# Paired landmark work, casts by DMA and earlier block sums in a fused attention and feed-forward kernel

## The chip, the cores and the metric

The kernel runs on one core of one Trainium2 chip. The metric is the device time in microseconds (us) of one execution; a profiled execution also has a span, from its first to its last recorded work. "PE" is TensorE, "PEld" its weight loads, "DVE" VectorE, "ACT" ScalarE, "POOL" GpSimd and "SP" SyncE, whose queue issues DMAs.

## The reference

Two stages. The first is an attention of eight batches, eight heads, 576 rows and 64 columns by landmarks (each the mean of 18 rows), with an iterated inverse:

```python
q_lm = q.reshape(B, H, 32, 18, D).mean(axis=3)
k_lm = k.reshape(B, H, 32, 18, D).mean(axis=3)
A, Bm, C = sm(q, k_lm), sm(q_lm, k_lm), sm(q_lm, k)   # softmax of scaled scores
Z = Bm.T / (norm1(Bm) * norminf(Bm) + 1e-06)          # per head
for _ in range(6):
    Z = 2 * Z - Z @ Bm @ Z
x = A @ Z @ C @ v                                     # heads side by side: (8, 576, 512)
```

The second takes `u = x + real(fft(fft(x, axis=1), axis=2))`, normalizes each row of u, and returns `u + max(un @ w_ch1, 0) @ w_ch2`, with w_ch1 of 512 x 2048 and w_ch2 of 2048 x 512.

## The kernel before

**Order of work.** The program first writes down every instruction as an `Op` with an assumed duration, a phase, a group and the tiles it touches (`Order.op`). `Order.solve` then plays the engines through in simulated time: on each engine the ready instruction with the smallest phase goes first, within a phase and batch the one with the longest chain behind it. The resulting order is issued as it stands, all of it through one line (L1324), which is why every row of the profile names that line; groups are told apart by tile names. Additions and subtractions issued through `self.E` may go to DVE or POOL, as the planner finds room.

**Tiles.** Buffers come from pools (`SLOTS`, L85; `BANKS`, L84). In the pools of `IN_ORDER`, "big" (8 tiles of 1280 columns) among them, a tile is given out only in the order in which the program wrote its uses down, whatever the phases say. "row" has 6 tiles; PSUM has 4 banks named "at", of which 2 are held for good from chunk 4 on. Two of the big tiles are held from then on as well, as a ring for block sums.

**Attention** (`attention`, L678) handles one batch in two groups of four heads. It loads k and q (two big tiles each), reduces them to landmark sums `lm` and a masked copy `qbd`, splits q into two fp16 halves, and calls `landmarks` (L943). That computes `Bm` for the eight heads, its norms, and six iterations (a bundle of 16 products of 32x32 blocks, a copy on ACT and an addition on DVE each); between them it calls `keys` and `values`, or from batch 2 (`LATE`) on `keys_turned` and `values_turned`, for C and C @ v. Their result becomes `Wx` and `Wt`. Then come A in three parts, its transposes by DMA, a transform over the rows, and `mix` (L1070), which forms u; `norm` (L1128) makes un and sends it through a DMA transpose into `unT`. Phases are 0 for batch 0 and 100 b for batch b.

**Feed-forward.** Two tiles of 128 rows are a chunk; a batch gives four tiles, and two batches a ninth from what is left. `chunk` (L1166), for chunks 0 to 3, multiplies by w1 (192 products into "hp", phase 1001) and by w2 (into "acc", phase 1000). All operands are two fp16 halves, three products for one. From chunk 4 (`SEVEN`) on `seven` (L1236) replaces the product with w2 by seven products of half blocks, for which `blocks_of` (L1204, phase 1000) has formed sums of w2's blocks and stored them in DRAM. The products of chunks fill whatever time attention leaves on PE. Until the first one, the planner fills PE with dummy products (`hp<-ones`).

**Weights** (`weights`, L597) are unpacked from 64-bit words to 16 tiles each: two ACT instructions, one DVE instruction, a product on PE for the scale, then scaling to `ws`, a cast to the high half (ACT) and a subtraction for the low half.

The block sums depend on one instruction, kept as `self.second`:

```python
if b == 1:
    self.second = self.order.ops[-1]
...
elif chunks == SEVEN - 1: self.order.gate = (self.second,)
```

Of the kernel before, what the change touches and what calls it, by code (L numbers as in the profile page):

```python
# [87 lines left out]
LINK, PATIENCE = 0.05, 0.0  # L88
SEVEN, RING, LATE, PORT, SPARE = 4, 10, 2, 0.05, 0.1
# [343 lines left out]
class Kernel:  # L433
# [77 lines left out]

    def turn(self, out, src):
# [84 lines left out]
    def weights(self):  # L597
# [7 lines left out]
        for w in range(2):  # L605
            gram = self.new("acc")
            for f in range(NF):
# [9 lines left out]
                half = dst.bitcast(BF16).rearrange("p (m x) -> p m x", x=2)[:, :, 1]  # L617
# [26 lines left out]
                for f2 in range(NF) if w else range(4 * g, 4 * g + 4):  # L644
# [6 lines left out]
                    self.A.copy(hi, src)  # L651
# [26 lines left out]
    def attention(self, b):  # L678
# [11 lines left out]
        lm = self.small([P, 2, 128], "lm", bufs=1)  # L690
        am = self.small(4, "amax")
        qbd = self.small([P, 4, 64], "qbd", bufs=1)
        qhs = []
        for g in range(2):
            kf, qf = loads[g][0][:, 0 : 2 * S], loads[g][1][:, 0:NQ]
            V.tensor_reduce(lm[:, g, 64:128], kf.rearrange("p (m t) -> p m t", t=18), AX.X, ALU.add)
            lv = lm[:, g, 0:64].rearrange("p (x o m) -> p x o m", o=2, m=8)
            qv = qf.rearrange("p (x o t) -> p x o t", o=2, t=2 * SEG)
            for o in range(2):
                V.tensor_reduce(lv[:, :, o], qv[:, :, o, o : o + 144].rearrange("p x (m t) -> p x m t", t=18), AX.X, ALU.add)  # L700
            qhs.append(self.big().bitcast(F16))
            A.activation(qhs[g][:, 0:NQ], qf, AF.Abs, accum_out=am[:, g : g + 1])
            V.tensor_tensor(
                qbd[:, 2 * g : 2 * g + 2].rearrange("p r (x m) -> p r x m", x=2),
                lm[:, g, 0:64].rearrange("p (r m) -> p r m", r=2).unsqueeze(2).broadcast_to([P, 2, 2, 32]),
                self.mask2.unsqueeze(1).unsqueeze(3).broadcast_to([P, 2, 2, 32]), ALU.mult,
            )
# [31 lines left out]
        land = self.landmarks(b, loads, qbd, lm)  # L739
# [77 lines left out]
        self.mix(b, ATs, CS, *land())  # L817

# [124 lines left out]
    def landmarks(self, b, loads, qbd, lm):  # L943
        mm, tr = self.mm, self.tr
        V, A = self.V, self.A
        small = self.small
        flat = lambda t: t.rearrange("p a b -> p (a b)")
        Bd = small([P, 2, 32], "Bd")
        R = small([P, 2, 64], "R")
        ps = self.at()  # L950
        self.together()
        for g in range(2):
            for pr in range(2):
                mm(ps[64 * pr : 64 * pr + 64, 32 * g : 32 * g + 32], qbd[:, 2 * g + pr], lm[:, g, 64 + 32 * pr : 96 + 32 * pr])
        self.apart()
        V.tensor_scalar(Bd.rearrange("p g m -> p (g m)"), ps[:, 0:64], 1.0 / 2592.0, None, ALU.mult)
        mx = small(2, "bmx")
        V.tensor_reduce(mx, Bd, AX.X, ALU.max)
        V.tensor_tensor(Bd, Bd, mx.unsqueeze(2).broadcast_to([P, 2, 32]), ALU.subtract)
        A.activation(Bd, Bd, AF.Exp)  # L960
        bs = small(2, "bs")
# [3 lines left out]
        nrm = small([P, 2, 3, 32], "nrm", bufs=1)  # L965
        V.tensor_tensor(nrm[:, :, 1, :], Bd, bs.unsqueeze(2).broadcast_to([P, 2, 32]), ALU.mult)
        rs = small(2, "rs")
        V.tensor_reduce(rs, nrm[:, :, 1, :], AX.X, ALU.add)
        V.tensor_tensor(
            nrm[:, :, 2, :], self.diag32.unsqueeze(1).broadcast_to([P, 2, 32]),  # L970
            rs.unsqueeze(2).broadcast_to([P, 2, 32]), ALU.mult,
        )

        Cs = self.keys(loads, qbd, lm) if b < LATE else self.keys_turned(loads, lm)

        psn = self.at()
        mm(psn[:, 0:128], flat(self.ones_bd), nrm[:, :, 1:3].rearrange("p g x m -> p g (x m)"))
        cm = small(4, "cm")
        V.tensor_reduce(cm, psn[:, 0:128].rearrange("p (x m) -> p x m", m=32), AX.X, ALU.max)
        ci = small(2, "ci")  # L980
# [4 lines left out]
        nci = small(2, "nci")  # L985
        V.tensor_scalar(nci, ci, -1.0, None, ALU.mult)
        BT = small([P, 2, 32], "BT", bufs=1)
        for g in range(2):
            V.transpose(BT[:, g], nrm[:, g, 1, :])
# [3 lines left out]
        for g in range(2):  # L993
# [3 lines left out]
        for g in range(2):  # L997
            V.scalar_tensor_tensor(nrm[:, g, 0, :], pse[:, 32 * g : 32 * g + 32], nci[:, g : g + 1], self.diag32, ALU.mult, ALU.add)
        (self.values if b < LATE else self.values_turned)(loads, Cs, ci, R)

        ES = nrm[:, :, 0:2].rearrange("p g x m -> p g (x m)")
        for it in range(6):
# [3 lines left out]
            for g in range(2):  # L1006
# [289 lines left out]
    def run(self):  # L1296
# [95 lines left out]
```

## Time and profile before

| | us |
|---|---|
| median of 3 runs | 958.4 (956.04 to 960.85) |
| the profiled execution | 957.02 |
| its span | 955.2 |
| PE busy | 923.6 (97%) |
| DVE busy | 760.7 (80%) |
| ACT busy | 490.1 (51%) |
| POOL busy | 225.1 (24%) |
| DMA | 128.27 MB, mean 134 GB/s |

PE's instructions overlap, so its busy time counts the end of one together with the start of the next; a bundle's cost is better read from its start to the start of what follows. An idle time in brackets is the engine's own, and the name behind it is what ended it. Busy shares over the whole span are means over stages of different kinds: weights and batch 0 (to about 70 us), weights with the first chunk, batch 1, block sums with batch 2, then seven-product chunks with attention beside them, and at the end chunks alone.

### The profile page before, as it was taken

The numbers are of one execution on the slowest core, as the hardware profiler recorded it, in microseconds if no ns is written. First come the engines' busy times: TensorE is split into PE (matmuls) and PEld (weight loads), VectorE is DVE, ScalarE is ACT, GpSimd is POOL, SyncE is SP. The second block draws the span as 40 slices with busy tenths as digits, with TensorE's granted clock in tenths as the row PEclk, the third lists the DMA queues.
The fourth block names the chain that finished last, engine by engine and source line by source line (L and its number), as shares of the span: only waits on it lengthen the run. The fifth ranks groups of instructions, "written<-read, shape, count | busy, mean of one in ns | idle before, by whom it ended". The sixth has DMA issues, their size and how long they took to land.

```text
span 955.2 us, 26527 instructions
## 1 busy us (share of the span) xinstructions
PE 923.6 (97%) x10730; PEld 747.6 (78%) x10730; DVE 760.7 (80%) x2012; ACT 490.1 (51%) x1031; POOL 225.1 (24%) x270
## 2 busy tenths in 40 slices
PE   8879899989999999999999999999999999999997
PEld 6668557656566888878888878888888888888886
DVE  7888996898998688898789987997698856865455
ACT  5899853245555444455454534564454633433332
POOL 0322010353552222140314211221242411301010
PEclk9999999999999999999999999999999999999999
DMA  9976110653735571557335552455535433334231
GB/s 347 302 245 210 58 33 17 161 128 79 258 116 149 110 200 54 155 118 197 108 100 155 136 168 66 119 142 134 178 101 155 121 87 95 101 116 116 79 106 50
DMA packets 166795, 128.27 MB, mean 134 GB/s; under 512 B 86416, under 2 KB 155536, under 8 KB 166544
## 3 DMA queue, kind: packets, MB, share of 16 engines
q1 hardware_dynamic: 166672, 126.57, 46.6%
q8 instruction: 84, 1.38, 0.6%
q14 instruction: 39, 0.32, 0.1%
HBM read 94.15 MB, written 14.68 MB: 114 GB/s over the span
## 4 chain that ended last, share of the span: by engine, by line
PE 65%; DVE 8%; DMA 4%; issue 1%; ACT 1%; SPq 1%; POOL 0%; DVEq 0%; ACTq 0%
PE hp L1324 30%; PE at L1324 19%; PE acc L1324 16%; DVE row L1324 2%; DMA big<-big 2%; DMA big<-q_dram 1%; DMA big<-sums 1%; DVE h L1324 1%; DVE big L1324 1%; SPq L1324 1%; DVE u L1324 1%; DVE lm L1324 1%; DVE sum L1324 1%; DMA big<-k_dram 1%; ACT big L1324 0%
## 5 line engine op out<-in xcount | busy, mean ns | idle before, releaser
L1324 PE MATMUL hp<-unT,w 128*128 128x256 f16 x3264 | 389.8, 273 | 0.6 <-DVE h L1324 0.6
L1324 PEld LDWEIGHTS <-w 128*128 128x128 f16 (+1 forms) x3584 | 343.3, 98 | 54.1 <-DVE w L1324 6.9
L1324 PEld LDWEIGHTS <-h 128*128 128x128 f16 x2604 | 247.7, 98 | 66.3 <-DVE h L1324 6.8
L1324 PE MATMUL acc<-w,h 128*128 128x256 f16 (+1 forms) x1260 | 199.3, 294 | 5.0 <-DVE h L1324 3.7
L1324 ACT ACTIVATE ws<-hp 128x512 f32<-128x512 f32 x112 | 66.8, 596 | 170.3 <-PE hp L1324 169.9
L1324 DVE TENSOR_TENSOR sum<-ws 128x256 f32<-128x256 f32 (+1 forms) x272 | 97.2, 402 | 71.4 <-ACT ws L1324 70.7
L1324 ACT CAST h<-sum 128x640 f16<-128x640 f32 x112 | 81.2, 725 | 79.2 <-DVE sum L1324 64.8
L1324 PE MATMUL at<-big,h 128*128 128x256 f16 x672 | 110.1, 273 | 0.0
L1324 POOL TENSOR_TENSOR sum<-ws 128x256 f32<-128x256 f32 (+1 forms) x64 | 44.2, 708 | 221.9 <-ACT ws L1324 193.6
L1324 DVE TENSOR_TENSOR h<-sum,h 128x640 f16<-128x640 f32 x86 | 71.4, 830 | 16.5 <-ACT h L1324 15.9
L1324 POOL TENSOR_TENSOR h<-sum,h 128x640 f16<-128x640 f32 x26 | 36.4, 1402 | 86.3 <-ACT h L1324 86.3
L1324 PE MATMUL acc<-big,h 128*128 128x256 f16 x336 | 55.0, 273 | 0.0
L1324 PE MATMUL at<-w,h 128*128 128x256 f16 x336 | 55.0, 273 | 0.0
L1324 ACT CAST row<-row 128x256 f16<-128x256 f32 (+1 forms) x76 | 36.6, 502 | 32.8 <-DVE row L1324 24.9
L1324 DVE TENSOR_REDUCE lm<-big 128x32 f32<-128x576 f32 (+1 forms) x48 | 44.3, 945 | 11.2 <-DMA big<-k_dram 8.1
L1324 PEld LDWEIGHTS <-big 128*128 128x128 f16 (+1 forms) x768 | 40.1, 99 | 9.0 <-issue 3.7
L1324 ACT CAST h<-ws 128x256 f16<-128x256 f32 x112 | 45.3, 405 | 2.8
L1324 DVE SCALAR_TENSOR_TENSOR u<-at,scw,row 128x128 f32<-128x128 f32 (+3 forms) x120 | 39.0, 387 | 7.8 <-PE at L1324 7.6
L1324 DVE TENSOR_TENSOR h<-ws,h 128x256 f16<-128x256 f32 x98 | 42.7, 435 | 0.4 <-ACT h L1324 0.4
L1324 ACT ACTIVATE big<-big 128x1168 f16<-128x1168 f32 (+1 forms) x26 | 25.4, 988 | 28.2 <-DMA big<-q_dram 18.6
L1324 DVE SCALAR_TENSOR_TENSOR u<-acc,winv,u 128x512 f32<-128x512 f32 x50 | 35.5, 742 | 4.4 <-PE acc L1324 4.3
L1324 POOL TENSOR_TENSOR r<-ve,mhalf 128x2 f32<-128x2 f32 (+1 forms) x20 | 15.6, 782 | 93.8 <-DVE ve L1324 93.5
(226 smaller groups left out, 1331.9 us busy)
## 6 DMA issues: line engine op xcount, KB each, us to landing
big<-sums SPq DMA_DIRECT2D x336, 128.0 KB, 2.2
w<-w_dram SPq DMA_DIRECT2D x22, 512.0 KB, 8.4
big<-q_dram SPq DMA_DIRECT2D x16, 584.0 KB, 6.0
big<-k_dram SPq DMA_DIRECT2D x16, 576.0 KB, 5.9
out_dram<-u SPq DMA_DIRECT2D x36, 256.0 KB, 2.3
big<-v_dram SPq DMA_DIRECT2D x12, 512.0 KB, 4.9
big<-w_dram SPq DMA_DIRECT2D x10, 512.0 KB, 6.2
sums<-row SPq DMA_DIRECT2D x40, 128.0 KB, 1.9
```

Source lines behind the costliest of these rows:

```text
L1324: getattr(engine, name)(*map(real, args), **{k: real(x) for k, x in kw.items()})
```

## The change

`landmarks` is divided. The sums of q and k become `landmark_sums`; Bm, the norms and the six iterations become `normed`, which takes one batch or two and lays them side by side in every tile; what is left of `landmarks` takes its result and runs keys and values behind it. `run` calls `ahead(3, 4)`, `ahead(5, 6)` and `ahead(7)` before batch 2, 4 and 6. `ahead` loads k and q of its batches (phase 100 b - 150, with b the first of them), forms their sums, and runs `normed` (phase 100 b - 50); the tiles of k and q are given back, and `attention` loads both again for its other uses. Batches 0 to 2 do the same work alone. Some small tiles have other numbers of buffers or move to "row".

In `weights`, the high half of every third tile of w1 is cast by a DMA issued on POOL's queue; for w2 the two unpacking instructions write in place of the raw words, and only the third writes the final tile. The block sums depend on the last instruction of batch 0.

```diff
+PULL, DRAW, PAIRS = 150, 50, (3, 5, 7)
...
+    def cast(self, out, src):
+        n = math.prod(src.shape) * mybir.dt.size(src.dtype)
+        self.order.op("POOL", 1.0, 2.3, [out], [src], (self.nc.gpsimd, "dma_start", (out, src), {}), nbytes=n)
...
-                dst, mag = slots[w][f], low.bitcast(F32) if w else self.new("h")[:, 0:512]
-                x = dst.bitcast(I32)
+                dst = slots[w][f].bitcast(I32)
+                x, mag = (low, top.bitcast(F32)) if w else (dst, self.new("h")[:, 0:512])
...
-                V.scalar_tensor_tensor(x, mag.bitcast(I32), 3, x, ALU.logical_shift_left, ALU.bitwise_or)
+                V.scalar_tensor_tensor(dst, mag.bitcast(I32), 3, x, ALU.logical_shift_left, ALU.bitwise_or)
...
-                    self.A.copy(hi, src)
+                    (self.A.copy if w or f2 % 3 else self.cast)(hi, src)
...
-        lm = self.small([P, 2, 128], "lm", bufs=1)
-        am = self.small(4, "amax")
-        qbd = self.small([P, 4, 64], "qbd", bufs=1)
+        am = self.small(4, "amax", bufs=4)
+        alone = b not in self.lms
+        if alone:
+            lm, qbd = self.landmark_sums(loads)
+        else:
+            lm = self.lms[b]
...
+        if alone:
+            self.normed_of[b] = (0, *self.normed([(lm, qbd)]))
...
-            AT = (self.mid(512).bitcast(F16) if u < 2 else self.small(256, "AT2", F16)).rearrange("p (c t) -> p c t", t=P)
-            hl = self.row(1024, F16) if u < 2 else self.small(256, "hl2", F16)
+            AT = (self.mid(512).bitcast(F16) if u < 2 else self.small(256, "AT2", F16, bufs=1)).rearrange("p (c t) -> p c t", t=P)
+            hl = self.row(1024, F16) if u < 2 else self.small(256, "hl2", F16, bufs=1)
...
+    def ahead(self, *batches):
+        b = batches[0]
+        self.set(100 * b - PULL, b, 2.0)
+        found = [self.landmark_sums(self.load(x)) for x in batches]
+        self.lms.update(zip(batches, (lm for lm, _ in found)))
+        self.set(100 * b - DRAW, b, 2.0)
+        made = self.normed(found)
+        for i, x in enumerate(batches):
+            self.normed_of[x] = (2 * i, *made)
+
+    def landmark_sums(self, loads):
+        lm = self.small([P, 2, 128], "lm", bufs=3)
+        qbd = self.row(256).rearrange("p (r m) -> p r m", r=4)
...
+    def normed(self, lms):
+        mm, V, A, small = self.mm, self.V, self.A, self.small
+        n = 2 * len(lms)
...
         for it in range(6):
             c0 = 0 if it < 5 else 32
             ps = self.at()
             self.together()
-            for g in range(2):
+            for g in range(n):
                 for i in blocks:
                     mm(ps[i, 64 * g + c0 : 64 * g + 64], ES[i, g, 0:32], ES[i, g, c0:])
             self.apart()
-            pv = ps[:, 0:128].rearrange("p (g m) -> p g m", g=2)
-            new = small([P, 2, 64], "ES", bufs=3)
+            pv = ps[:, 0 : 64 * n].rearrange("p (g m) -> p g m", g=n)
             if it < 5:
+                new = small([P, 2, 64], "ES", bufs=2) if n == 2 else self.row(256).rearrange("p (g m) -> p g m", g=4)
                 A.copy(new[:, :, 0:32], pv[:, :, 0:32])
...
+    def landmarks(self, b, loads, lm, x, last, ci, keys, values):
+        last, ci = last[:, x : x + 2], ci[:, x : x + 2]
+        values(loads, keys(), ci, R)
...
         for b in range(self.NB):
+            if b + 1 in PAIRS:
+                self.ahead(*range(b + 1, min(b + 3, self.NB)))
             self.attention(b)
-            if b == 1:
+            if b == 0:
                 self.second = self.order.ops[-1]
```

## Rows read from the trace of the kernel before

**Rows 1.** The page of the profile: the span, the busy time of each engine, and the TensorE clock in 40 equal slices (tenths of full speed).

```profile
span 955.2 us, 26527 instructions
...
PE 923.6 (97%) x10730; PEld 747.6 (78%) x10730; DVE 760.7 (80%) x2012; ACT 490.1 (51%) x1031; POOL 225.1 (24%) x270
...
PEclk9999999999999999999999999999999999999999
```

**Rows 2.** Busy time by stage. Columns: stretch in us from the span's start, its length, then the busy us (and instructions) of PE, PE's weight loads, DVE, ACT and POOL, the granted clock, the mean busy share of the DMA engines, GB/s.

```profile
72.00:112.00 40.00, 36.30 (x344) 29.98 (x342) 35.36 (x81) 36.60 (x70) 5.93 (x7) 0.97 0.53 159
112.00:192.00 80.00, 79.48 (x842) 49.04 (x842) 65.48 (x172) 35.73 (x79) 13.57 (x15) 0.98 0.26 67
192.00:300.00 108.00, 102.18 (x1183) 67.81 (x1180) 99.12 (x265) 54.81 (x135) 48.47 (x60) 1.00 0.51 144
300.00:945.00 645.00, 641.59 (x7506) 551.58 (x7504) 495.69 (x1297) 303.04 (x622) 141.86 (x167) 1.00 0.45 123
```

**Rows 3.** TensorE in order of time, 56 to 130 us: start, duration, what, and in brackets the idle time before it and what ended it. The first row is the first multiplication of chunk 0; the last is the first product with w2.

```profile
70.87 8.38 PE L1324 MATMUL hp<-unT,w 128*128 128x256 f16 x60
...
94.51 0.41 PE L1324 MATMUL acc<-w 128*128 128x128 bf16 x4 [0.61 <-DVE w L1324]
...
111.92 3.02 PE L1324 MATMUL acc<-w,mt 128*128 128x512 f16 x6 [1.48 <-ACT w L1324]
```

**Rows 4.** The same view, 120 to 310 us: two products of h with w2 in chunk 1.

```profile
196.83 2.33 PE L1324 MATMUL acc<-w,h 128*128 128x512 f16 x10 [1.18 <-DVE h L1324]
...
201.86 2.33 PE L1324 MATMUL acc<-w,h 128*128 128x512 f16 x10 [1.33 <-DVE h L1324]
```

**Rows 5.** ScalarE in order of time, 36 to 76 and 76 to 130 us: the casts of w1's tiles 0 (46.17), 2 and 3 (50.32), two later ones with the instruction behind them, and tile 12's (86.96).

```profile
46.17 0.61 ACT L1324 CAST w<-ws 128x512 f16<-128x512 f32 x1
...
50.32 1.16 ACT L1324 CAST w<-ws 128x512 f16<-128x512 f32 x2
...
67.54 1.12 ACT L1324 CAST w<-ws 128x512 f16<-128x512 f32 x2
68.57 0.67 ACT L1324 ACTIVATE big<-big 128x512 f32<-128x512 f32 x1
...
86.96 0.63 ACT L1324 CAST w<-ws 128x512 f16<-128x512 f32 x1
```

**Rows 6.** DMA issues by kind: out<-in, queue, operation, count, KB of each, median us from issue to landing.

```profile
sums<-row SPq DMA_DIRECT2D x40, 128.0 KB, 1.9
...
big<-k_dram SPq DMA_DIRECT2D x16, 576.0 KB, 5.9
```

**Rows 7.** Groups of instructions by shape (the sums of a batch's q, its k, and the masked copy): count, busy us, mean ns of one, idle time of the engine before them.

```profile
L1324 DVE TENSOR_REDUCE lm<-big 128x32 f32<-128x576 f32 x32 | 23.0, 745 | 3.0 <-DMA big<-q_dram 3.0
...
L1324 DVE TENSOR_REDUCE lm<-big 128x64 f32<-128x1152 f32 x16 | 21.5, 1347 | 8.2 <-DMA big<-k_dram 8.1
...
L1324 DVE TENSOR_TENSOR qbd<-lm,mask 128x128 f32<-128x128 f32 x16 | 5.7, 370 | 0.1
```

**Rows 8.** The same view: the additions of the iteration, five per batch.

```profile
L1324 DVE TENSOR_TENSOR ES<-ES,at 128x64 f32<-128x64 f32 x40 | 8.4, 210 | 3.5 <-ACT ES L1324 2.4 <-PE at L1324 0.9
```

**Rows 9.** TensorE in order of time: one bundle of the iteration and what follows it (219.85), a bundle of 24 products with Wt (41.72) and a doubled one (260.59), each with what follows.

```profile
219.85 0.43 PE L1324 MATMUL at<-ES 32*32 32x64 f32 x16
220.21 4.11 PE L1324 MATMUL hp<-big,w 128*128 128x256 f16 x36
...
41.72 0.57 PE L1324 MATMUL at<-t,Wt 64*32 64x262 f16 x24
42.23 0.28 PE L1324 MATMUL hp<-ones 128*128 128x256 f16 x1
...
260.59 0.86 PE L1324 MATMUL at<-t,Wt 64*32 64x262 f16 x48
261.38 1.48 PE L1324 MATMUL hp<-unT,w 128*128 128x256 f16 x12
```

**Rows 10.** Groups by shape: the larger parts of the block sums (the sum of a tile's halves, sums of its blocks, their low halves), on VectorE and on GpSimd.

```profile
L1324 DVE TENSOR_TENSOR row<-row 128x256 f16<-128x256 f32 x23 | 12.8, 573 | 0.2 <-ACT row L1324 0.2
...
L1324 POOL TENSOR_TENSOR row<-row 128x256 f16<-128x256 f32 x17 | 12.0, 716 | 23.6 <-ACT row L1324 23.6
...
L1324 POOL TENSOR_TENSOR ws<-w 128x512 f32<-128x512 f16 x11 | 14.3, 1309 | 0.1
...
L1324 POOL TENSOR_TENSOR row<-ws,ws 128x256 f32<-128x256 f32 x15 | 11.7, 782 | 9.4 <-ACT ml L1324 5.4 <-DVE ws L1324 3.9
...
L1324 DVE TENSOR_TENSOR row<-ws,ws 128x256 f32<-128x256 f32 x9 | 3.9, 458 | 0.0
```

**Rows 11.** The SyncE queue in order of time, 0 to 320 us: the first and the last load of k and q of batch 2, and the transpose of its first tile of un.

```profile
178.03 0.57 SPq L1324 DMA_DIRECT2D big<-k_dram  x1
...
185.05 0.42 SPq L1324 DMA_DIRECT2D big<-q_dram  x1
...
283.30 1.28 SPq L1324 DMA_TRANSPOSE unT<-row  x1
```

**Rows 12.** TensorE in order of time: the first multiplication of chunk 4 (each chunk has 192, counted from 70.87).

```profile
301.39 2.79 PE L1324 MATMUL hp<-unT,w 128*128 128x256 f16 x24
```

**Rows 13.** SyncE's transpose of batch 3's rest tile, and TensorE's product that reads batch 2's.

```profile
304.97 1.20 SPq L1324 DMA_TRANSPOSE AT<-hl  x1
...
311.43 0.44 PE L1324 MATMUL at<-Wx,AT 64*64 64x64 f16 x16
```

More of the change, by code (lines that the diff above doesn't have):

```diff
@@ L510, in dma @@
         self.order.ops[-1].name = "dma"
+    def cast(self, out, src):
+        n = math.prod(src.shape) * mybir.dt.size(src.dtype)
+        self.order.op("POOL", 1.0, 2.3, [out], [src], (self.nc.gpsimd, "dma_start", (out, src), {}), nbytes=n)
+        self.order.ops[-1].name = "dma"
     def turn(self, out, src):
@@ L689, in attention @@
         NQ = 16 * SEG
-        lm = self.small([P, 2, 128], "lm", bufs=1)
-        am = self.small(4, "amax")
-        qbd = self.small([P, 4, 64], "qbd", bufs=1)
+        am = self.small(4, "amax", bufs=4)
+        turned = b >= LATE
+        alone = b not in self.lms
[3 more added lines that the diff above has]
+            lm = self.lms[b]
         qhs = []
         for g in range(2):
[L695 to L700, printed above, removed]
-            qhs.append(self.big().bitcast(F16))
[L702 to L707, printed above, removed]
+            qhs.append(self.big().bitcast(F16))
+            A.activation(qhs[g][:, 0:NQ], loads[g][1][:, 0:NQ], AF.Abs, accum_out=am[:, g : g + 1])
         V.tensor_reduce(am[:, 2:4], lm[:, :, 64:128], AX.X, ALU.add, apply_absolute_value=True)
@@ L737, in attention @@
             V.tensor_copy(scr[64 * g : 64 * g + 64], sc[64 * g : 64 * g + 64, 4 + g : 5 + g])
-        land = self.landmarks(b, loads, qbd, lm)
+        if alone:
+            self.normed_of[b] = (0, *self.normed([(lm, qbd)]))
+        if not turned:
+            land = self.landmarks(b, loads, lm, *self.normed_of[b], lambda: self.keys(loads, qbd, lm), self.values)
+        else:
+            land = self.landmarks(b, loads, lm, *self.normed_of[b], lambda: self.keys_turned(loads, lm), self.values_turned)
         aes = []
@@ L817, in attention @@
         self.mix(b, ATs, CS, *land())
+    def ahead(self, *batches):
[8 more added lines that the diff above has]
+    def landmark_sums(self, loads):
+        V = self.V
+        lm = self.small([P, 2, 128], "lm", bufs=3)
+        qbd = self.row(256).rearrange("p (r m) -> p r m", r=4)
+        for g in range(2):
+            kf, qf = loads[g][0][:, 0 : 2 * S], loads[g][1][:, 0 : 16 * SEG]
+            V.tensor_reduce(lm[:, g, 64:128], kf.rearrange("p (m t) -> p m t", t=18), AX.X, ALU.add)
+            lv = lm[:, g, 0:64].rearrange("p (x o m) -> p x o m", o=2, m=8)
+            qv = qf.rearrange("p (x o t) -> p x o t", o=2, t=2 * SEG)
+            for o in range(2):
+                V.tensor_reduce(lv[:, :, o], qv[:, :, o, o : o + 144].rearrange("p x (m t) -> p x m t", t=18), AX.X, ALU.add)
+            V.tensor_tensor(
+                qbd[:, 2 * g : 2 * g + 2].rearrange("p r (x m) -> p r x m", x=2),
+                lm[:, g, 0:64].rearrange("p (r m) -> p r m", r=2).unsqueeze(2).broadcast_to([P, 2, 2, 32]),
+                self.mask2.unsqueeze(1).unsqueeze(3).broadcast_to([P, 2, 2, 32]), ALU.mult,
+            )
+        return lm, qbd
     def keys(self, loads, qbd, lm):
@@ L984, in landmarks @@
         V.reciprocal(ci, ci)
-        nci = small(2, "nci")
+        nci = several(1, "nci")
         V.tensor_scalar(nci, ci, -1.0, None, ALU.mult)
-        BT = small([P, 2, 32], "BT", bufs=1)
-        for g in range(2):
+        BT = small([P, 4, 32], "BT", bufs=1)
+        for g in range(n):
             V.transpose(BT[:, g], nrm[:, g, 1, :])
@@ L992, in landmarks @@
         self.together()
-        for g in range(2):
+        for g in range(n):
             for i in blocks:
@@ L996, in landmarks @@
         self.apart()
-        for g in range(2):
+        for g in range(n):
             V.scalar_tensor_tensor(nrm[:, g, 0, :], pse[:, 32 * g : 32 * g + 32], nci[:, g : g + 1], self.diag32, ALU.mult, ALU.add)
-        (self.values if b < LATE else self.values_turned)(loads, Cs, ci, R)
         ES = nrm[:, :, 0:2].rearrange("p g x m -> p g (x m)")
@@ L1005, in landmarks @@
             self.together()
-            for g in range(2):
+            for g in range(n):
                 for i in blocks:
@@ L1018, in landmarks @@
             self.E.tensor_tensor(
[L1019 removed]
+                nbd[:, g].rearrange("p i (d m) -> p i d m", d=2), last[:, g].unsqueeze(1).unsqueeze(1).broadcast_to([P, 4, 2, 32]),
                 self.mask4.unsqueeze(2).unsqueeze(3).broadcast_to([P, 4, 2, 32]), ALU.mult,
```

57 lines of the change are left out of this document (30 added, 27 removed).

## The prediction

> **What bounds the kernel now.** I read the busy line and the clock slices first, then the stages, then TensorE's (PE's) waits in each stage. PE is busy 923.6 of 955.2 us and its clock stays at the upper level, 2.4 GHz, nearly throughout [rows 1]. The stage table says where the rest lies. PE's idle time is 3.7 us in 72 to 112, 0.5 in 112 to 192, 5.8 in 192 to 300 and 3.4 in the 645 us from 300 to 945 [rows 2]: 13.4 us in all. Before that, PE fills with dummy products until the first multiplication of a chunk at 70.87 [rows 3]; nothing behind it can be done earlier than that point allows. So the kernel after 70.87 is a PE queue that hardly ever runs dry. DVE with 77% and ACT with 47% of the last long stage [rows 2] are not the bound; their saved microseconds count only where PE waited for them. The price of this change is therefore read from 72 to 300, plus whatever it takes out of PE's own queue.
>
> Two waits stand in that stretch. In 72 to 112 ACT is busy 36.6 of 40 us [rows 2], unpacking and splitting the weights, and PE waits for it: 0.61 for an unpacked tile at 94.51 and 1.48 at 111.92 for the first tile of w2, among shorter ones [rows 3]. In 192 to 300 DVE is busy 99.1 of 108 us [rows 2], and PE waits 1.18 and 1.33 us for h, which a late DVE instruction makes [rows 4].
>
> **The change part by part.** The sum is made in the profiled execution's time, 957.0 us (span 955.2 and 1.8 around it); the median of the runs shown, 958.4, stands 1.4 above it, and I add that at the end.
>
> *Casts by DMA.* Tiles 0, 3, 6, 9, 12 and 15 of w1 lose their cast on ACT. Two casts run from 67.54 and the next instruction starts at 68.57 [rows 5]: 0.515 each, so 6 x 0.515 = 3.1 us less on ACT, from the first at 46.17 on. The chunk's start at 70.87 I leave where it is: it waits for the transposed tiles of batch 0, whose chain goes ahead of weight work in the planner. Behind it, w2 comes up to 3.1 us earlier and the idle time of 72 to 112 shrinks; all of it is 3.7, nothing is 0. Two of the six, tiles 0 and 3, are cast before 52 us [rows 5], where I count only a part of the time as brought forward, so I take 2.3. The new cost is a wait: the low half (DVE or POOL) waits for a DMA in place of ACT. No row has a casting DMA; by the nearest ones it lands 1.9 us (128 KB, on chip) to 5.9 us (a big load) after its issue [rows 6], against 0.5 for the cast. Queued behind its issue on POOL are other low halves and the powers of the norm. Tiles 0 and 3 are cast 20 us before the chunk starts and have that to spare; tile 12, cast at 86.96 [rows 5] while chunk 0 is already running, may have none, worth 0 to 5.9 - 0.5 = 5.4 us once. I cost it at 0, covered by the chunk multiplications that are held for lack of h buffers anyway. That w2's unpacking no longer writes into the final slot first only removes a wait of ACT; it is in the 2.3.
>
> DVE is busy 35.4 of the 40 us in which most of the casts fall [rows 2]. The Trainium skill, "SBUF — State Buffer", section "SBUF: two separate sides", speaks against this part: a DMA issued from GpSimd has its descriptors written by GpSimd, and a DVE instruction in a two-port mode locks it out meanwhile, so that the DMA looks stalled. The trace of before has no such DMA and can't show it. By that rule most of the 2.3 would be spent again, and the sum would be near -4; that is rival 4.
>
> *Block sums beside batch 1.* They depend on the last instruction of batch 0 instead of batch 1. Their larger groups are 16.7 us of DVE and 38.0 us of POOL [rows 10]; they now begin after batch 1 and crowd into 192 to 300. In 112 to 192 DVE has 80 - 65.5 = 14.5 us free, and POOL 66 [rows 2]; w2 is complete only near 127. I let some 10 us of DVE go there. Their phase number is behind batch 1's, so what they cost it is at most the rest of one instruction per hop, beside a PE that idles 0.5 us in 80.
>
> *Sums ahead of batches 3 and 4.* Per batch DVE has two reductions of 1.347, four of 0.745 and two masks of 0.370 [rows 7], 6.4 us; for both batches 12.8. Batch 3's were in 192 to 300 already, batch 4's are new there. So DVE in 192 to 300: -10 + 6.4 + some 4 for the part of the paired chain that batch 4 brings forward, an estimate: nearly nothing. I take 1.5 us of the 5.8 for the better spread (bounds: 5.8 gained, or as much lost if the new sums delay h as the old ones did).
>
> *One pass for a pair.* Elementwise instructions of two batches become one of twice the width. An update of the iteration is 64 columns in 0.210 us [rows 8]; mostly fixed time. That is some 20 DVE instructions saved per pair, 4 us each time, but beside a PE that waits little: I give it 0.5 of the 3.4 us after 300 (0 to 3.4). On PE itself: 16 small products take 220.21 - 219.85 = 0.36 us, and they pay the drain once per bundle. The nearest doubled bundle: 24 products with Wt take 42.23 - 41.72 = 0.51, 48 take 261.38 - 260.59 = 0.79 [rows 9], so a merge saves 0.23. The lower end is nothing, if PE issues the second half at the full price. Nine bundles per pair (scores, norms, squares, six steps), two pairs: 18 x 0 to 0.23, 0 to 4.1; I take 0.12 each, 2.2. Batch 7 goes alone and saves nothing.
>
> *Loads.* Batches 3 to 7 read q and k twice, 20 more DMAs of 0.58 MB on SP. What matters is that big tiles are given out in emission order: the eight tiles for 3 and 4 come before batch 2's. Batch 2's loads were issued from 178.03 to 185.05 [rows 11]. Eight loads are 4.6 MB; 159 GB/s at a share of 0.53 [rows 2] makes 300 at full use, 15.5 us, and batch 2's own four another 7.7. So its last q lands near 178 + 23 = 201 in place of 185.05 + 6 = 191: 10 us late, with transposes and loads of sums queued behind on SP. What absorbs it: batch 2's first tile was transposed at 283.30 [rows 11], lands within the bounds of rows 6, say 3 us later, and chunk 4, which needs it, started at 301.39 [rows 12]: 15 us spare, and the lighter DVE shortens batch 2. I cost it +0.5 (0 to 13, by rival 1).
>
> *Single buffers for the rest tile.* Batch 3's transpose into AT2 at 304.97 came before the product that reads batch 2's at 311.43 [rows 13]; with one buffer it must follow. Its reader is the last part of batch 3's mix, so 0.
>
> Sum: -2.3 - 1.5 - 0.5 - 2.2 + 0.5 = -6.0; 957.0 - 6.0 = 951.0, and on the scale of the median 952.
>
> **The rivals** (on the scale of the median).
> 1. *Batch 2 too late: slower.* If the loads and the 12.8 us of sums don't overlap, and the paired chain, some 24 small instructions of 0.21 [rows 8] or 5 us of DVE, gets in between, batch 2 slips 10 + 12.8 + 5 = 28 us, 13 beyond the spare 15, and PE starves at the start of chunk 4, near 300. With the other gains, 6.5 less the 1.5 of DVE's relief that it cancels, it is 958.4 + 13 - 5 = 966. It decides from a slip of 15 us on; slower by more than 0.5% needs one of 25. For it: the strict order of big tiles, and DVE at 92% in that stretch. Against it: fewer block sums there, and a planner that sees the transfers.
> 2. *Moved, not removed.* PE reaches 192 earlier and waits there that much longer, since DVE now has sums of three batches at once. Half the merging gain is left: 957. For it: DVE's load in rows 2 hardly falls on balance.
> 3. *All of it.* The idle time of 72 to 945 goes (12.9 without 112 to 192), with the full 4.1 of merging: 941. Against it: short waits of varied causes rarely all go.
> 4. *The casts stall* behind DVE, which is busy 35.4 of 40 us [rows 2]. Each cast then waits for one or two instructions of 0.7 to 1.35 us, w1's low halves come late, and the 2.3 is lost with another 0.5: 955.
>
> **How the numbers follow.** Forecast 952 (its own range 948 to 956) 0.42; rival 1 0.17; rival 2 0.22; rival 3 0.12; rival 4 0.07. A change of 0.5% is 4.8 us, about what a measurement can tell from none: below 953.6 and above 963.2 on the median's scale. Faster: four fifths of the forecast, rival 3 and a little of rival 4, 0.47. Slower: rival 1, which lies past 963.2 with nearly all of its spread, and the tail of rival 2, 0.19. The rest, 0.34. The range leaves out most of rival 3 and the far half of rival 1, some 0.2 in all: 944 to 966.
>
> **What would show it.** Casts: idle PE in 72 to 112 down from 3.7 to about 1.5, and the first product with w2 near 110. Block sums: stores of sums beginning near 130, during batch 1. Loads: batch 2's last q landing near 201; the first multiplication of chunk 4 no later than 301, without a wait of PE ahead of it. Merging: bundles of 32 products in under 0.7 us. After 300, the same PE busy time per chunk. Wrong if the first chunk starts more than 2 us from 70.87, if PE is idle for over 8 us in 192 to 320, or if PE's count of useful work changes by more than 4 us.

## The result, and the profile after

The changed kernel takes 968.4 us (median of 5 runs, 964.4 to 969.4) against 958.4 before: ratio 1.0092, interval 1.0071 to 1.0113. It is slower by 0.9%, and outside the range. The profiled execution is the fastest of the five, 964.4 us.

The page's span and busy line, as in [rows 1]:

```profile
span 962.6 us, 26566 instructions
PE 920.3 (96%) x10727; PEld 748.5 (78%) x10727; DVE 743.6 (77%) x1959; ACT 484.6 (50%) x1013; POOL 245.1 (25%) x289
```

DVE lost 17 us of work and ACT 5.5, and the span grew by 7.4 us. Not all of DVE's relief is work saved: POOL gained 20 us against [rows 1], in part because additions that may run on either went there (its `h<-ws,h` rose from 14 to 23, its `h<-sum,h` from 26 to 31). The stages, with the columns of [rows 2]:

```profile
72.00:112.00 40.00, 37.12 (x346) 29.71 (x345) 36.05 (x73) 33.19 (x60) 8.39 (x11) 1.00 0.59 169
112.00:192.00 80.00, 70.04 (x789) 43.55 (x788) 74.58 (x194) 42.82 (x104) 39.01 (x47) 0.97 0.30 88
192.00:300.00 108.00, 106.50 (x1309) 72.42 (x1309) 84.57 (x236) 45.71 (x108) 29.22 (x38) 0.98 0.52 158
300.00:945.00 645.00, 635.12 (x7351) 547.09 (x7350) 480.35 (x1250) 300.18 (x608) 148.04 (x169) 1.00 0.48 136
```

PE's idle time is 2.9, 10.0, 1.5 and 9.9 us, 24.2 in all before rounding, against 3.7, 0.5, 5.8 and 3.4, 13.4 in all [rows 2]. Two of the four stages improved; 112 to 192, which had hardly any idle time to lose, now has 10. PE's list says where (idle time ahead of an instruction stands in brackets, with its releaser):

```profile
182.41 1.47 PE L1368 MATMUL hp<-unT,w 128*128 128x256 f16 x12
193.24 2.72 PE L1368 MATMUL hp<-big,w 128*128 128x256 f16 x12 [9.36 <-DMA big<-row]
...
313.00 1.09 PE L1368 MATMUL acc<-w,h 128*128 128x256 f16 x6 [3.30 <-ACT row L1368]
```

The first is the end of chunk 1; the second the first multiplication of chunk 2, which needs the second transposed tile of batch 1. One wait of 9.36 us stands there where the kernel before had none above 2 us anywhere after 72. The chain of waits through that point (start, length, what):

```profile
180.52 3.11 DMA big<-row
...
185.44 7.75 DMA big<-row
193.24 2.72 PE hp L1368 x12
```

Two transposes by DMA, the same work, land after 3.11 and after 7.75 us. SP's queue has what lies between them:

```profile
180.52 1.23 SPq L1368 DMA_TRANSPOSE big<-row  x1
181.85 0.53 SPq L1368 DMA_DIRECT2D big<-k_dram  x1
182.47 1.23 SPq L1368 DMA_TRANSPOSE unT<-row  x1
183.75 0.58 SPq L1368 DMA_DIRECT2D big<-q_dram  x1
184.39 0.47 SPq L1368 DMA_DIRECT2D big<-k_dram  x1
184.95 0.39 SPq L1368 DMA_DIRECT2D big<-q_dram  x1
185.44 2.29 SPq L1368 DMA_TRANSPOSE big<-row  x1
```

The kernel before issued the same two transposes here, with two loads between them:

```profile
175.31 1.23 SPq L1324 DMA_TRANSPOSE big<-row  x1
...
178.03 0.57 SPq L1324 DMA_DIRECT2D big<-k_dram  x1
178.69 0.39 SPq L1324 DMA_DIRECT2D big<-q_dram  x1
179.17 1.53 SPq L1324 DMA_TRANSPOSE big<-row  x1
```

So the second transpose is issued 6.3 us later (185.44 against 179.17; the first one 5.2), and it stands behind more. Four loads of 0.58 MB in front of it are 2.3 MB; the rows at the end of this text show 335 GB/s at that time, so they need 6.9 us. The last of the four landed at 192.2, the transpose at 193.2. Against a clear way, 3.1 us, the queue costs it 4.6.

The kernel before did not have a clear way either. The landing of its second transpose is not in the trace, but the loads in front of it landed 4.5 and 5.8 us after their issue, the later one at 184.5. If the transpose followed 1.0 us behind, as in the changed kernel, it was there near 185.5 (an estimate), 0.8 us before chunk 2 began at 186.31. The tile then comes 7.7 us later, 6.3 of them by its issue and 1.4 by the queue, and PE has ended chunk 1 at 183.9 in place of 186.3 and stands there 2.4 us sooner: 7.7 + 2.4 - 0.8 = 9.3, the wait.

The Trainium skill, "DMA: Bandwidth & Descriptors", section "Queues, rings and completion order", says that a DMA queue has one ring per DMA engine, and that each engine takes the descriptors of a ring in order; SP's transfers all stand in one queue in this profile, and the trace agrees with a transpose that waits behind what was issued before it.

The wait at 313 is of the same family. In ACT's list

```profile
310.30 0.62 ACT L1368 CAST row<-row 128x512 f16<-128x512 f32 x1 [4.31 <-DMA unT<-row]
310.83 0.40 ACT L1368 CAST h<-ws 128x256 f16<-128x256 f32 x1
311.13 0.72 ACT L1368 CAST h<-sum 128x640 f16<-128x640 f32 x1
```

a cast waits 4.31 us for a transpose to free its buffer, and the two casts of h that PE needs stand behind it, in the order that the planner wrote down.

### The profile page after: what moved, and what is told of

Read it like the earlier page. It is cut to its first block, busy times and chain, and to the rows that moved or that the text cites. A ratio compares the mean times of both kernels' runs of the same rounds, so it can differ in the third digit from the quotient of the medians.

```text
span 962.6 us, 26566 instructions
## 1 busy us (share of the span) xinstructions
PE 920.3 (96%) x10727; PEld 748.5 (78%) x10727; DVE 743.6 (77%) x1959; ACT 484.6 (50%) x1013; POOL 245.1 (25%) x289
## 4 chain that ended last, share of the span: by engine, by line
PE 64%; DVE 14%; ACT 8%; DMA 6%; issue 5%; POOL 1%; SPq 0%; DVEq 0%; ACTq 0%; POOLq 0%
PE hp L1368 28%; PE at L1368 19%; PE acc L1368 17%; DVE u L1368 2%; DVE row L1368 2%; ACT big L1368 2%; DMA big<-big 2%; ACT w L1368 1%; DVE h L1368 1%; DMA unT<-row 1%; ACT row L1368 1%; DVE sum L1368 1%; ACT ws L1368 1%; DMA big<-row 1%; DVE big L1368 1%
## 5 line engine op out<-in xcount | busy, mean ns | idle before, releaser
L1368 DVE TENSOR_TENSOR sum<-ws 128x256 f32<-128x256 f32 (+1 forms) x264 | 93.7, 403 | 76.8 <-ACT ws L1368 76.4
L1368 POOL TENSOR_TENSOR sum<-ws 128x256 f32<-128x256 f32 (+1 forms) x72 | 50.3, 716 | 302.0 <-ACT ws L1368 235.4
L1368 DVE TENSOR_TENSOR h<-sum,h 128x640 f16<-128x640 f32 x81 | 66.6, 822 | 16.0 <-ACT h L1368 15.5
L1368 POOL TENSOR_TENSOR h<-sum,h 128x640 f16<-128x640 f32 x31 | 44.0, 1419 | 101.7 <-ACT h L1368 101.5
L1368 DVE TENSOR_TENSOR h<-ws,h 128x256 f16<-128x256 f32 x89 | 38.7, 435 | 3.8 <-ACT h L1368 3.6
L1368 ACT ACTIVATE big<-big 128x1168 f16<-128x1168 f32 (+2 forms) x36 | 31.6, 904 | 19.4 <-PE at L1368 9.4
L1368 PEld LDWEIGHTS <-mt 64*128 64x128 f16 (+1 forms) x752 | 27.5, 96 | 12.6 <-issue 6.2
```

The lines of the kernel that those rows point to most:

```text
L1368: getattr(engine, name)(*map(real, args), **{k: real(x) for k, x in kw.items()})
```

## The experiments

Two causes were set against each other, and against the prediction's own steps: that the block sums beside batch 1 make its last instructions late, and that the loads (of the pass ahead, or any) stand before the transposes in the DMA queue. In the expectations the first is also called S and the second R.

### Parts of the change undone

*a_sums_late*: the block sums wait for batch 1 again.

```diff
-            if b == 0:
+            if b == 1:
                 self.second = self.order.ops[-1]
```

> The changed kernel with one part undone: the block sums depend on the last instruction of batch 1 again. PE's wait ahead of chunk 2 was 9.4 us. Theory S (block sums hold up batch 1's chain, so that its first transposes are issued 5 to 6 us later): batch 1's two transposes for chunk 2 are issued near 175 and 179 again, the wait falls to 3 to 4 us, but 192 to 300 gets back some idle time; time 962 to 965. Theory R (the transposes stand behind the loads for batches 3 and 4 in the DMA rings): the second transpose still takes 7 to 8 us from issue to landing and the wait stays at 5 us or more; time 964 to 968. If neither matters (pairing or casts cost the time), the wait stays at 9 us.

Measured 979.9 us, ratio 1.0203 (1.0162 to 1.0244): slower still, and above both ranges. Its transposes were issued at 174.64 and 177.96, and chunk 2 began at 184.57 without a wait. PE's list shows what came in its place:

```profile
193.78 2.72 PE L1368 MATMUL hp<-big,w 128*128 128x256 f16 x12 [3.81 <-DVE h L1368]
...
851.44 3.78 PE L1368 MATMUL hp<-unT,w 128*128 128x256 f16 x17 [7.46 <-DMA unT<-row]
```

So the early block sums do make the first transpose 6 us late, and the second 7.5. But with them back behind batch 1 other waits cost more than they did: besides the two shown PE waits 4.64 us at 312.4 for a transpose, ahead of chunk 4, and others of 1.5 to 2 us near 410.

*b_no_pair34*: batches 3 and 4 go alone, as before.

```diff
-PULL, DRAW, PAIRS = 150, 50, (3, 5, 7)
+PULL, DRAW, PAIRS = 150, 50, (5, 7)
```

> The changed kernel without the pass ahead for batches 3 and 4, which do their landmark work alone; 5 and 6, and 7, keep theirs, and the block sums stay beside batch 1. Theory R: only batch 2's own loads are around the transposes, the second one lands within 3 to 4 us, and the wait ahead of chunk 2 falls from 9.4 to 3 to 5 us; time 961 to 964. Theory S: the transposes are issued at 180 and 185 as before and the wait stays at 7 us or more; time 966 to 969. Against both: no change in the wait.

Measured 970.0 us, 1.0105 (1.0070 to 1.0140). Its longest waits:

```profile
193.01 2.29 PE L1368 MATMUL hp<-big,w 128*128 128x256 f16 x10 [9.21 <-DMA big<-row]
...
843.01 2.29 PE L1368 MATMUL hp<-unT,w 128*128 128x256 f16 x10 [7.48 <-DMA unT<-row]
```

The wait ahead of chunk 2 is the same without the pass ahead: batch 2's own loads stand before the transpose, which lands 7.60 us after its issue. For this wait it made no difference whose four loads stood there. The like times do not say that the pass for 3 and 4 is free: the wait near 843, which the changed kernel does not have, came with the new list.

*c_both*: both edits together, which leaves the casts and the pass for 5 and 6.

> Both undone together: block sums after batch 1, no pass ahead for 3 and 4. What is left of the change is the casts, the in-place unpacking, and the passes ahead for 5 and 6, and 7. If S and R together make the loss, the wait ahead of chunk 2 is gone (under 1 us), w2 is ready near 108 as in the changed kernel, and the time is 952 to 957, below the kernel before. If the casts or the pairing cost time by themselves, it is 962 or more.

Measured 958.2 us, 0.9980 (0.9964 to 0.9997). That lies between the two forecasts. Chunk 2 starts at 185.97 without a wait; then PE waits 4.71 us at 196.09 for h, because ACT's list stands still for a late load of q, issued at 185.82 and 7.72 us on its way:

```profile
193.56 1.18 ACT L1368 ACTIVATE big<-big 128x1168 f16<-128x1168 f32 x1 [3.38 <-DMA big<-q_dram]
194.64 0.19 ACT L1368 ACTIVATION_READ_ACCUMULATOR big<-big 128x1 f32 x1
194.74 0.58 ACT L1368 ACTIVATE h<-hp 128x512 f16<-128x512 f32 x1
```

That wait alone is longer than what the casts were forecast to bring.

### One part alone on the kernel before

*d_before_sums*: only the block sums' gate is moved. *h_before_casts*: only the six casts go by DMA.

```diff
-            if b == 1:
+            if b == 0:
...
-                    self.A.copy(hi, src)
+                    (self.A.copy if w or f2 % 3 else self.cast)(hi, src)
```

> The kernel before, with the block sums beside batch 1 and nothing else of the change. Theory S: batch 1's first transposes are issued 4 to 6 us later than 175 and 179, and land behind loads; PE waits 4 to 8 us ahead of chunk 2, and the idle time of 192 to 300 falls from 5.8 to about 2; time 960 to 964. If the block sums are harmless by themselves and the loss is in the pass ahead, the time is 955 to 958 and there is no such wait.

> The kernel before with the six casts of w1 by DMA and nothing else. ACT has 3.1 us less work; the first product with w2 comes at 109 to 110 in place of 111.9, PE's idle time in 72 to 112 falls by about 1 us, the time is 955 to 958 (before: 958.4 to 960). If the casts wait for DVE and are late, w2 is no earlier and the time is 959 to 962.

Measured 962.2 us, 1.0033 (1.0016 to 1.0051), and 961.5 us, 1.0024 (1.0006 to 1.0042). Each has one new wait above 2 us. In the first, of PE for the transpose, again ahead of chunk 2; its two transposes were issued at 184.02 and 189.70, 8.7 and 10.5 us later than before, with the gate as the only edit:

```profile
197.00 3.36 PE L1324 MATMUL hp<-big,w 128*128 128x256 f16 x15 [5.59 <-DMA big<-row]
```

and in the second, though its first product with w2 comes at 108.56 in place of 111.92:

```profile
198.43 1.80 PE L1329 MATMUL hp<-big,w 128*128 128x256 f16 x8 [5.00 <-DVE h L1329]
```

Three microseconds won near 110 do not reach the end. In this list, too, ACT stands still for the last q load of batch 2, which is issued at 188.18 in place of 185.05 and lands at 195.9 in place of 190.4, and h comes behind it. The time lies in the range given for late casts (959 to 962), though w2 was early. Neither expectation on idle time held: in the first kernel 192 to 300 has 6.5 us of it, not some 2, and in the second 72 to 112 has 4.1, not 1 less than 3.7.

### The loads and the transposes

*e_loads_after*: in the plan, the loads of the pass ahead of 3 and 4 wait for the two transposes that chunk 2 needs.

```diff
-        found = [self.landmark_sums(self.load(x)) for x in batches]
+        made_in = self.unT[2].tile if b == 3 else None
+        self.order.gate = [o for o in self.order.ops if o.name == "turn" and made_in in o.tiles]
+        loads = [self.load(x) for x in batches]
+        self.order.gate = ()
+        found = [self.landmark_sums(x) for x in loads]
```

> The changed kernel, whose loads ahead for batches 3 and 4 wait until the two transposes for chunk 2 have landed (a dependency written into the planner's list; all else as in the change). Theory R: both transposes land within 3 to 4 us of their issue, the wait ahead of chunk 2 falls to 3 to 5 us, and batch 2's loads move back by some 4 us without a wait of PE; time 960 to 964. Theory S: the issue times stay at 180 and 185, the wait stays at 7 us or more; time 966 to 970.

Measured 975.3 us, 1.0157 (1.0126 to 1.0188), above both ranges. The second transpose, issued at 185.12, landed after some 3.1 us, and the wait fell to 4.30; another came, by its side:

```profile
188.22 2.74 PE L1372 MATMUL hp<-big,w 128*128 128x256 f16 x12 [4.30 <-DMA big<-row]
...
205.72 4.23 PE L1372 MATMUL acc<-w,h 128*128 128x512 f16 x12 [3.93 <-ACT h L1372]
```

A wait of 7.47 us at 845.4 came too, as in the two runs above: the gate had changed the whole plan behind it. So *i_sp_order* left every list as it was, but for SP's: after planning, the loads between the two transposes go behind the second.

```diff
+    def transposes_first(self, done):
+        made_in = self.unT[2].tile
+        turns = [i for i, o in enumerate(done) if o.name == "turn" and made_in in o.tiles]
+        late = [i for i in range(turns[0], turns[1]) if done[i].name == "dma" and done[i].nbytes > 400000]
+        keep = [o for i, o in enumerate(done[: turns[1] + 1]) if i not in late]
+        return keep + [done[i] for i in late] + done[turns[1] + 1 :]
...
-            for o in self.order.solve():
+            for o in self.transposes_first(self.order.solve()):
```

> The changed kernel with every engine's list of instructions as it was, except SP's: the four loads of k and q that stood between the two transposes for chunk 2 are moved behind the second one. Theory R (that transpose took 7.75 us because the loads stand before it in the DMA rings): it lands about 3 us after its issue near 185, PE's wait ahead of chunk 2 falls from 9.4 to 4 to 5 us, and the time is 962 to 966, where the changed kernel has 968.4. If something else keeps it (the transpose itself, the un tile), the wait stays at 8 us or more and the time at 968.

Measured 967.7 us, 1.0082 (1.0055 to 1.0109), the changed kernel's own time and not the 962 to 966 expected. PE's list:

```profile
189.55 2.74 PE L1376 MATMUL hp<-big,w 128*128 128x256 f16 x12 [4.45 <-DMA big<-row]
...
202.60 2.58 PE L1376 MATMUL hp<-big,w 128*128 128x256 f16 x12 [3.60 <-DVE h L1376]
```

and the chain between the two:

```profile
187.75 2.69 DMA big<-k_dram
190.45 9.59 DMA unT<-row
...
200.17 0.73 POOL row L1376
...
201.23 0.60 ACT h L1376
201.85 0.69 DVE h L1376
```

That shows both halves of the queue's part. With the loads out of its way the transpose, issued at 186.43, releases PE at 189.55, 3.1 us later, and the wait falls by 4.9 us. And the next transpose now stands behind the loads for 9.59 us, a POOL instruction waits for it, an ACT cast for POOL's buffer, and h for ACT: 3.60 of the 4.9 us are lost again ten microseconds on.

### A planner that sees the queue

The planner gives every other DMA its bytes and queues it behind those in flight; a transpose it gives none, so in its plan it lands after a fixed time. It had the second transpose of chunk 2 land at 181.0, 2.5 us after its issue. One edit gives it its bytes:

```diff
         self.order.op("SP", 1.15 + 0.016 * blocks, 1.25, [out], [src],
-            (self.nc.sync, "dma_start_transpose", (out, src), {}))
+            (self.nc.sync, "dma_start_transpose", (out, src), {}), nbytes=math.prod(src.shape) * 2)
```

It was put on the kernel with both edits undone (*l_c_pipe*), on the kernel before (*m_before_pipe*), on the whole changed kernel (*f_after_pipe*), and on it with one edit undone: late block sums (*a_late_pipe*) or no pass for 3 and 4 (*b_no_pair34_pipe*).

> The kernel with both parts undone (block sums after batch 1, no pass ahead for 3 and 4; 958.2 in its run), planned with one more fact: a transpose takes its turn in the DMA rings behind the loads issued before it, where the planner had let it land 1.25 us after its issue ended whatever stood ahead. If transposes behind loads are what the plans miss, the order it finds has no wait over 3 us for a transpose, and the time is 950 to 956. If the waits for h at 196 (DVE and ACT held in order behind a late load of q) come from elsewhere, they stay, and the time is 957 to 960.

> The kernel before, with nothing changed except that the planner counts a transpose's bytes as queued behind the loads, as it does for every other DMA. The planner's own end of the whole list is then 946.4 us, against 935.0 when it thought the transposes free, with planned gaps of PE of 3.5 us near 110 and of 8.4 us near 815. Theory 'the plan was blind' (the transposes that come late on the chip are the difference between plan and chip): the time is the plan's end plus about 10 us, as in the run with both parts undone and the same model (935.5 planned, 945.6 measured), so 954 to 959 with PE waiting some 5 us near 825 and nowhere near 193; no faster than before, because the old list has no place to hide the late transposes. Rival 'a lucky list' (that run's gain is chance, and any new list scatters by some 10 us around the old time): anything from 948 to 970, with waits at other places than the planned ones.

> The changed kernel, whole, planned with the transposes queued behind the loads. The planner's end is 944.0 us, with gaps of PE of 2.7 us at 184.7 and 6.1 us at 193.4, both ahead of work of chunk 2. Theory 'the plan was blind': 944.0 + 10, so 952 to 957, some 13 us faster than the changed kernel; the wait ahead of chunk 2 stays, as 6 to 9 us in one or two pieces between 184 and 200, since the block sums still delay batch 1's transposes; the 3.3 us near 313 goes. Rival 'the block sums cost it, and the rest is noise': 963 to 972, with the wait near 193 and the one near 313 both still there.

> The changed kernel with the block sums back behind batch 2's start (gated on batch 1, as before), planned with the transposes queued behind the loads. The planner's end is 950.1 us: no gap of PE between 112 and 285, but five gaps, 14 us together, between 290 and 309, where chunk 4 waits for batch 2 (the place of the prediction's first rival). Theory 'the plan was blind': 950.1 + 10, so 958 to 963, with 10 to 16 us of PE's waits between 288 and 315. The prediction's rival 1 (batch 2 late at chunk 4) would then be shown as what the block sums beside batch 1 were needed to avoid. Rival 'a lucky list': no waits there above 5 us in all.

> The changed kernel without the pass ahead of batches 3 and 4 (they go alone, as before), block sums beside batch 1, planned with the transposes queued behind the loads. The planner's end is 939.2 us, with gaps of PE of 2.5 us at 184.6 and 1.5 us at 188.6. Theory 'the plan was blind': 939.2 + 10, so 947 to 952, with 3 to 6 us of waits between 183 and 200 and none above 3 us near 845. Set beside the run with both parts undone (945.6), this prices the block sums' move at 2 to 6 us, and beside the whole changed kernel under the same model it prices the pass ahead of 3 and 4 at 3 to 7 us. Rival 'the block sums cost it': within 0.5% of the whole changed kernel under the same model.

The planner's own end of the list, without and with the transposes' bytes, beside what was measured (us; ratio to the kernel before):

```
                               plan   measured         plan with bytes   measured
before                         935.0  958.4            946.4             962.5 (1.0030)
whole change                   935.7  968.4 (1.0092)   944.0             957.9 (0.9972)
no pass for 3 and 4            943.3  970.0 (1.0105)   939.2             951.1 (0.9898)
block sums late                951.3  979.9 (1.0203)   950.1             970.8 (1.0106)
neither of the two             932.4  958.2 (0.9980)   935.5             945.6 (0.9858)
```

The chip is 23 to 33 us behind the old plans and 10 to 21 behind the new ones. Both rank their five kernels as the chip does, but the old one made the change 0.7 us dearer, where it measured 10. Of the expected times, that of the whole change (952 to 957) and of the one without the pass (947 to 952) came to within 1 us, with waits of about the planned size ahead of chunk 2. The kernel with both undone (950 to 956) came 4 us below, the kernel before (954 to 959) 4 us above, and the one with late block sums (958 to 963) 8 us above; its waits came at chunk 4 as planned, but near 307 to 325 in place of 288 to 315. The rival, that a new list scatters by chance, has the order and the places against it; that some microseconds of each step are luck is not excluded, since each of these kernels is one list.

The last column's best, 945.6 us, 0.9858 (0.9822 to 0.9894), is faster than both kernels. The queue is not gone there: its second transpose for chunk 2 still lands 7.4 us after its issue at 181.07, behind three loads. But the list has products for PE until then, and chunk 2 begins at 188.49 without a wait. Its stages:

```profile
112.00:192.00 80.00, 78.09 (x844) 48.22 (x842) 64.89 (x175) 35.87 (x80) 8.97 (x12) 1.00 0.25 62
192.00:300.00 108.00, 107.57 (x1258) 73.02 (x1256) 102.56 (x275) 61.15 (x152) 58.08 (x74) 1.00 0.58 152
```

PE idles 0.4 us in 192 to 300 beside a DVE that is busy 102.6 of 108: a heavy load of DVE in that stage, which the prediction wanted to lighten, does not by itself hold PE up. With the whole change under the new plan the wait ahead of chunk 2 remains, in pieces, 7.6 us, and the one near 313 is gone:

```profile
189.36 0.61 PE L1368 MATMUL acc<-w,h 128*128 128x512 f16 x2 [1.34 <-ACT h L1368]
190.97 2.33 PE L1368 MATMUL acc<-w,h 128*128 128x512 f16 x10 [1.00 <-DVE h L1368]
...
198.51 1.89 PE L1368 MATMUL hp<-big,w 128*128 128x256 f16 x8 [5.21 <-DMA big<-row]
```

From 945.6 to 951.1 is the price of the early block sums, 5.5 us; from there to 957.9 that of the pass for 3 and 4, 6.8. The 945.6 comes from another chip than the rest; by the ratios, each to the kernel before on its own chip, the two prices are some 4 and 7 us. With the pass the second transpose for chunk 2 lands 10.5 us after its issue, without it 7.8. Alone, with the block sums late, the pass costs 25.2 (970.8 less 945.6; 24 by the ratios), by the mechanism of the prediction's rival 1: batch 2 comes late, and PE has nothing ahead of chunk 4, which begins at 324.91 when batch 2's transpose lands:

```profile
314.32 3.36 PE L1368 MATMUL at<-kbd,big 128*128 128x64 f16 x60 [7.51 <-DVE kbd L1368]
...
324.91 1.44 PE L1368 MATMUL hp<-unT,w 128*128 128x256 f16 x6 [4.26 <-DMA unT<-row]
```

The kernel before loses 0.3% by the new plan. It gets a wait of 3.05 us at 113.87, for ACT, and a longer one for batch 7, which the plan had at 817.5 with 5.5 us:

```profile
834.57 1.65 PE L1324 MATMUL hp<-unT,w 128*128 128x256 f16 x7 [7.46 <-DMA unT<-row]
```

It was 7.46 to 7.48 us long in four kernels here, this one, a_sums_late, b_no_pair34 and e_loads_after, and in none of the others. So part of the difference between two of these kernels is whether their list has it.

## Why the prediction was wrong

**Block sums, -1.5: the step that failed.** The prediction let 10 us of DVE go into 112 to 192 because DVE had 14.5 free there, and costed the delay of batch 1 at "at most the rest of one instruction per hop, beside a PE that idles 0.5 us in 80". That PE was busy in chunk 1 is no cover for batch 1's results, which chunk 2 needs. The spare time was computed for chunk 4 (15 us) and not for the consumer next in line: before, the second transpose was issued at 179.17, landed near 185.5 by the estimate above, and chunk 2 began at 186.31, so less than 1 us was spare. The sums took DVE to 74.6 of 80 us, and the second transpose was issued 6.3 us later. The delay stands in the planner's own list already: with nothing but the gate moved (d_before_sums) it issues the second transpose at 178.4 in place of 173.8. Which hops of batch 1's chain make it up was not resolved. In 192 to 300 idle time did fall by 4.3 us (5.8 to 1.5), more than forecast, but behind a wait that had already held PE back.

**Loads, +0.5: right place of attention, wrong consumer.** Chunk 4 began its first multiplication at 302.57 without a wait, so its 15 us did cover batch 2, though the last of the twelve q and k loads was issued only at 203.72 and, at some 7 us each, landed near 211 in place of the 201 forecast. What was missed is the transposes "queued behind on SP", named in that sentence and priced only in chunk 4's spare. Against a clear way that queue costs chunk 2 4.6 us, which i_sp_order took away there; 1.4 of them, by the estimate, are new with the change. The pass for 3 and 4, whose terms in the sum come to a gain, costs some 7 us where the planner sees the queue (f_after_pipe against b_no_pair34_pipe). No run prices the wait ahead of chunk 2 by itself: i_sp_order took 4.9 us of it away and was 0.7 us faster, and every other edit made a new list with waits of its own.

**Casts, -2.3.** The mechanism came: the first product with w2 at 108.02, 3.9 us sooner than [rows 3], in place of 110 as forecast; idle time in 72 to 112 fell only to 2.9, not 1.5. A cast took 5.5 us from issue to landing (median of six, from 2.3 to 9.2; three of them are above the bound of 5.9); the one wait of 3.32 us that it caused, in POOL near 54, lay under cover. Rival 4 did not happen: its price, a late w2, does not show. Whether a locked GpSimd, which the Trainium skill, "SBUF — State Buffer", section "SBUF: two separate sides", gives reason to fear, is part of the longer landings, no run here shows. But the gain is not one of the whole kernel: alone it measured 1.0024, with its 5.0 us wait of PE at 198.

**Merging, -2.2.** Right as far as it was measured. Two bundles of the iteration in the changed kernel, with what follows each:

```profile
240.59 0.43 PE L1368 MATMUL at<-row 32*32 32x64 f32 x16 [0.27 <-ACT big L1368]
240.95 1.47 PE L1368 MATMUL acc<-w,h 128*128 128x512 f16 x6
...
244.09 0.65 PE L1368 MATMUL at<-row 32*32 32x64 f32 x32
244.68 1.47 PE L1368 MATMUL acc<-w,h 128*128 128x512 f16 x6
```

16 products take 0.36 us to the next, 32 take 0.59: 0.13 saved per merge, 0.12 taken, and 18 times 2.3 us if all nine bundles of a pair save as much. In the balance, 10.8 us more idle time and 7.4 more span leave 3.4 us less of other PE time, which holds these 2.3; the rest was not assigned.

**DVE's relief after 300, -0.5.** Idle time rose from 3.4 to 9.9 there: 3.30 at 313, and 1.76 at 405.9 for a transpose and 1.46 at 664.1 for h.

**The rivals.** Rival 2, "moved, not removed", had the place and the direction right ("PE reaches 192 earlier and waits there that much longer") and the price wrong, 957 in place of 968: it let what was won be lost, and had no queue to add to it. Rival 1, the slower one, came close in time (966) by a mechanism that this kernel does not have: its chunk 4 is not starved. It is real where the block sums stay late: 4.64 us ahead of chunk 4 in a_sums_late, and in a_late_pipe some 25 us in all where 13 were worked out. The stores of sums, from 132.17 (130 forecast), and the bundles under 0.7 us were right. The sign that was to show it wrong, over 8 us of idle PE in 192 to 320, was looked for a few microseconds too late: the wait stands from 183.9 to 193.2.

## What to carry to other kernels

When work moves into a stage where an engine has free time, take each consumer of that stage's results in order of time, the next one first, and work out its spare: when its last input lands, and when it is wanted. Ask of a transfer what was issued before it in its queue: here the same transpose took 3.1 us or 7.8, and the order of an engine's list carries such a delay on to products that need none of its data. Where a planner writes the lists, what it does not model is the first thing to look for: one argument more was worth 9 to 19 us to the four kernels with parts of the change, and cost the kernel before 0.3%.

## What the runs showed that was not expected

Two long waits of PE cost more here than their length. The stretch around the wait ahead of chunk 2 in the changed kernel (columns of [rows 2]):

```profile
187.00:193.20 6.20, 0.00 (x0) 0.00 (x0) 4.83 (x8) 0.81 (x2) 3.32 (x4) 0.51 1.05 335
193.20:197.20 4.00, 3.96 (x16) 2.31 (x16) 0.00 (x0) 0.81 (x2) 2.16 (x4) 0.50 1.11 399
```

PE had been idle since 183.9; the granted clock fell to the lower level, 1.2 GHz, and stayed there for the first 4 us of work, in which twelve products took 2.72 us that take 1.47 otherwise. That is some 2 us on top of the 9.36. In a_late_pipe, after its 7.51 and 4.26 us, it is dearer:

```profile
310.00:330.00 20.00, 10.78 (x119) 6.68 (x119) 14.01 (x37) 6.20 (x14) 3.98 (x3) 0.50 0.71 145
```

10.8 us of work at half the clock cost about 5.4 more, an estimate, near half of what the planner, which has no clock, missed by more in this kernel (20.7 us behind its plan) than in l_c_pipe (10.1). In l_c_pipe the clock averaged 0.999.
